# Contracting over 64-row tile pairs instead of 128-row passes in a fused attention and gated-FFN kernel

## The chip, the cores and the metric

The kernel runs on one core of one Trainium2 chip. Times are device microseconds of one execution. The numbers of a table or a sentence come from fast runs unless it says otherwise.

## The reference, cut to what matters

```python
# x: 2048 tokens x 576, bf16; 32 heads of 18; window of 256 keys, causal
xn = layernorm(x)
q, k, v = split(xn @ wqkv)                     # wqkv: 576 x 1728
o = softmax(mask(q @ k.T * 18**-0.5)) @ v      # per head
s = o @ wo                                     # wo: 576 x 576
h = sigmoid(xn @ w_gate) * (xn @ w_up)         # 576 x 4608 each
out = x + s * silu(h @ w_down)                 # w_down: 4608 x 576
```

The width 576 is what the change is about. It is four and a half times 128, so a contraction over it does not fill the kernel's passes of 128 rows (128\*128 in the profile's shapes) a whole number of times. It is nine times 64.

## The kernel before

A Python program builds a graph of operations, a list scheduler fixes their order on each engine from estimated durations, and the engines are ordered by semaphores. The tokens are processed in four chunks of 512. The attention of one chunk is interleaved with the FFN of the chunk before. Five ways of contracting matter here.

Gate/up takes two blocks of 128 columns at a time. Each block has four passes over 128 rows for gate and four for up. The remaining 64 rows are done as a pair of 64-row tiles: gate's on rows 0 to 63 of the array, up's on rows 64 to 127, at the same time (the two start 3 ns apart in the trace) and into two PSUM banks.

```python
for kt in range(4):                                     # main(): 128 rows
    eng.matmul(bank(h, w), wgs[:, sw, 4*w + kt, fc], x_in[:, kt, :], ...)
for w in range(2):                                      # rem(): 2 x 64 rows
    r = slice(64*w, 64*w + 64)
    eng.matmul(bank(h, w), wgs[r, sw, 8, fc], x_in[r, 4, :], ..., tile_position=(64*w, 0))

for fa in range(0, NFT, 2):                             # two blocks, fa and fb
    main(fa, ha, 0, True, ha); main(fa, ha, 1, True, None)
    rm = pe(..., rem of fa and rem of fb, [], hb)       # one piece, takes fb's PSUM unit
    tail(fa, ha, rm, rm)                                # tanh on ACT, product on DVE
    g = main(fb, hb, 0, ...); u = main(fb, hb, 1, ...)
    tail(fb, hb, g, u)
# ... cut
```

The projections q/k, v and wo pad 576 to five passes of 128 rows, with zeroed weights in the last one. V and wo have 576 output columns, done as 512 + 64. PV contracts 128 keys per pass into 19 columns. The down projection has 36 full passes of 128 rows per token block, each as 512 + 64 columns. The scores contract 18 rows per head and use four row tiles of 32 rows at once (in the trace all four start within 10 ns).

The softmax here doesn't subtract the row's maximum and nothing guards it: scores larger than these inputs give would overflow.

Of the kernel before, what the change touches and what calls it, by code (L numbers as in the profile page):

```python
# [13 lines left out]
KT = 5  # L14
# [12 lines left out]
UNIT = 18  # L27
NUNIT = 2 * H
NVB = 8
NQS = 4  # L30
NEX = 4
NXR = 4
# [11 lines left out]
def mm_ns(n):  # L44
    return max(25.0, n / 2.4 + 2.7)


def act_ns(n):
    return n / 1.2 + 175.0

# [53 lines left out]
class Op:  # L104
    __slots__ = ("eng", "est", "deps", "fn", "name", "prio", "start", "end", "tok", "needs_tok",
                 "nbytes", "idx", "succs", "cidx", "odeps", "acq", "lane")

    def __init__(self, eng, est, fn, name, deps, prio, nbytes, odeps, acq):
# [27 lines left out]
        self.lane = None  # L136
        for d in self.odeps:
            assert d.eng == eng
# [22 lines left out]
class Builder:  # L161
# [32 lines left out]
    def alloc_memory(self):  # L194
# [17 lines left out]
        self.xnT, _ = seq("xnT", [P, 2, KT, NT])  # L212
# [6 lines left out]
        self.kT, _ = seq("kT", [P, 2, NHG, NT])  # L219
        self.expr, zex = seq("expr", [P, NEX, 4, NT])  # L220
        self.stage = nc.alloc_sbuf_tensor_at("stage", [P, KT, 2 * D], bf16, offset=zex)
        assert size([P, KT, 2 * D], bf16) <= size([P, NEX, 4, NT], bf16)
        self.o_tok, _ = seq("o_tok", [P, BPC * D + 64])
        self.oT, _ = seq("oT", [P, 2, KT, P])
        self.s_attn, _ = seq("s_attn", [P, 2 * BPC, D])
        self.wqk, _ = seq("wqk", [P, KT, 2 * D])
        self.wv_sb, _ = seq("wv_sb", [P, KT, D])
        self.wo_sb, _ = seq("wo_sb", [P, KT, D])
        self.qd, _ = seq("qd", [P, NQD, 2, NT])
        self.xr, _ = seq("xr", [P, NXR, D])  # L230
        self.xnr, _ = seq("xnr", [P, NXN, KT * P])
# [8 lines left out]
        self.rstd, _ = seq("rstd", [P, NST, 1], f32)  # L240
        self.rrec, _ = seq("rrec", [P, 2, 4 * BPC], f32)
# [7 lines left out]
    def build_graph(self):  # L249
# [6 lines left out]
        self.r_rec = Ring(2, "rrec")  # L256
        self.r_oT = Ring(2, "oT")
# [24 lines left out]
        for c in range(NC):  # L282
            self.build_ln(c)
            self.build_v(c)
            made = 0
            for hg in range(NHG):
                need = min(NQK, (8 * UNIT * (hg + 2) - 1) // (2 * P) + 1)
                while made < need:
                    self.build_qk(c, made)
                    made += 1  # L290
                self.build_attn(c, hg)
            self.build_wo(c)
            self.build_ffn(c)

    def load_x(self, c):
        for i in range(0, BPC, 2):
            st = c * BPC + i
            slots, dd = [], []
            for _ in range(2):
                s_, d_ = self.r_xr.produce()  # L300
                slots.append(s_)
                dd += d_
            assert slots[1] == slots[0] + 1
            if c == 0:
                for j in range(2):
                    self.x_dma[st + j] = (self.dma(self.xr[:, slots[j], :], self.x[(st + j) * P:(st + j + 1) * P, :],
                                                   P * D * 2, f"dma:x{st + j}", ("x0", st + j), prio=0), slots[j])
            else:
                o = self.dma(self.xr[:, slots[0]:slots[0] + 2, :],
                             self.x[st * P:(st + 2) * P, :].rearrange("(t p) d -> p t d", p=P),  # L310
                             2 * P * D * 2, f"dma:x{st}", ("x", slots[0]), deps=dd, prio=0)
                for j in range(2):
                    self.x_dma[st + j] = (o, slots[j])

    def build_consts(self):
# [6 lines left out]
        z1 = op("POOL", 400, lambda e: e.memset(self.wqk[64:128, KT - 1, :], 0.0), "init:wqkz", deps=[self.op_ident], prio=1)  # L322
        z2 = op("POOL", 400, lambda e: e.memset(self.wv_sb[64:128, KT - 1, :], 0.0), "init:wvz", deps=[z1], prio=1)
        z3 = op("POOL", 400, lambda e: e.memset(self.wo_sb[64:128, KT - 1, :], 0.0), "init:woz", deps=[z2], prio=1)
        self.op_vones = op("POOL", 600, lambda e: e.memset(self.v_aug[:, :, :, DH:DH + 1], 1.0), "init:vones", deps=[z3], prio=1)
        self.op_opad = op("POOL", 200, lambda e: e.memset(self.o_tok[:, BPC * D:], 0.0), "init:opad", deps=[self.op_vones], prio=1)
        o2 = op("POOL", 500, lambda e: e.memset(self.mask[:, :, :], 1.0), "init:m0", deps=[self.op_opad], prio=1)
        ms = [o2]
        for i in range(4):
# [3 lines left out]
            else:  # L333
# [5 lines left out]
        sa = self.dma(self.stage[:, 0:4, :], self.wqkv[0:512, 0:2 * D].rearrange("(kt p) c -> p kt c", p=P),  # L339
                      4 * P * 2 * D * 2, "dma:stage", ("stage", 0), prio=2)  # L340
        sb = self.dma(self.stage[0:64, 4, :], self.wqkv[512:576, 0:2 * D], 64 * 2 * D * 2, "dma:stage4",
                      ("stage", 1), prio=2)
        va = self.dma(self.wv_sb[:, 0:4, :], self.wqkv[0:512, 2 * D:3 * D].rearrange("(kt p) c -> p kt c", p=P),
                      4 * P * D * 2, "dma:wv", ("wv", 0), prio=2)
        vb = self.dma(self.wv_sb[0:64, 4, :], self.wqkv[512:576, 2 * D:3 * D], 64 * D * 2, "dma:wv4",
                      ("wv", 1), prio=2)
        self.op_wv = [va, vb, z2]
        wa = self.dma(self.wo_sb[:, 0:4, :], self.wo[0:512, :].rearrange("(kt p) c -> p kt c", p=P),
                      4 * P * D * 2, "dma:wo", ("wo", 0), prio=8)
        wb = self.dma(self.wo_sb[0:64, 4, :], self.wo[512:576, :], 64 * D * 2, "dma:wo4", ("wo", 1), prio=8)  # L350
        self.op_wo_w = [wa, wb, z3]
        self.op_wqk = [z1]
        for kt in range(KT):
            def f_pack(eng, kt=kt):
                rows = P if kt < KT - 1 else 64
                dst = self.wqk[0:rows, kt, :].rearrange("p (g w c) -> p w g c", w=2, c=72)
                src = self.stage[0:rows, kt, :].rearrange("p (w g c) -> p w g c", w=2, g=NHG)
                return eng.activation(dst, src, ACTF.Copy)
            self.op_wqk.append(op("ACT", act_ns(2 * D), f_pack, f"pack:{kt}", deps=[sa if kt < 4 else sb], prio=2))

    def build_ln(self, c):
        op = self.op
        xs = c % 2
        if c > 0:
            self.load_x(c)
        war = self.xnT_rel[c - 2] if c >= 2 else []
        for i in range(BPC):
            st = c * BPC + i
            o_x, sx = self.x_dma[st]
            ss, ds = self.r_st.produce()  # L370
            b1 = op("DVE", 430, lambda e, ss=ss, sx=sx: e.bn_stats(self.bnst[:, ss, 0, :], self.xr[:, sx, 0:288]),
                    f"ln:bn1:{st}", deps=[o_x, ds], prio=0)
            b2 = op("DVE", 430, lambda e, ss=ss, sx=sx: e.bn_stats(self.bnst[:, ss, 1, :], self.xr[:, sx, 288:576]),
                    f"ln:bn2:{st}", deps=[o_x, ds], prio=0)
            ag = op("DVE", 200, lambda e, ss=ss: e.bn_aggr(self.mv[:, ss, :], self.bnst[:, ss, :, :]),
                    f"ln:ag:{st}", deps=[b1, b2], prio=0)
            ve = op("DVE", 140, lambda e, ss=ss: e.tensor_scalar(self.veps[:, ss, :], self.mv[:, ss, 1:2], EPS, None,
                                                                ALU.add), f"ln:ve:{st}", deps=[ag], prio=0)
            rs = op("POOL", 560, lambda e, ss=ss: e.tensor_tensor(self.rstd[:, ss, :], self.veps[:, ss, :],
                                                                  self.neghalf[:, :], ALU.pow),  # L380
                    f"ln:rs:{st}", deps=[ve, self.op_negh], prio=0)
            sn, dn = self.r_xn.produce()
            ap = op("DVE", 430, lambda e, ss=ss, sx=sx, sn=sn: e.tensor_scalar(
                self.xnr[:, sn, 0:D], self.xr[:, sx, :], self.mv[:, ss, 0:1], self.rstd[:, ss, :],
                ALU.subtract, ALU.mult), f"ln:ap:{st}", deps=[rs, ag, dn], prio=0)
            dup = op("DVE", 110, lambda e, sn=sn: e.tensor_copy(self.xnr[:, sn, D:KT * P], self.xnr[:, sn, 4 * P:D]),
                     f"ln:dup:{st}", deps=[ap], prio=0)
            self.r_xr.release(sx, ap)
# [3 lines left out]
            def f_tr(eng, h=h, sn=sn):  # L392
                b = h.units[0] * 2048
                res = None
                for kt in range(KT):
                    res = eng.transpose(self.psb[:, b + kt * P:b + (kt + 1) * P], self.xnr[:, sn, kt * P:(kt + 1) * P],  # L396
                                        self.ident[:, :])
                return res
            tr = op("PE", 5 * 60, f_tr, f"tr:{st}", deps=[dup, self.op_ident, war], prio=0, acq=h)
            self.r_xn.release(sn, tr)  # L400

            def f_xe(eng, h=h, i=i, xs=xs):
                b = h.units[0] * 2048
                src = self.psb[:, b:b + 5 * P].rearrange("p (k c) -> p k c", k=KT)
                return eng.activation(self.xnT[:, xs, :, i * P:(i + 1) * P], src, ACTF.Copy)
            xe = op("ACT", act_ns(5 * P), f_xe, f"xe:{st}", deps=[tr], prio=0)
            h.release(xe)
            self.op_xnT[c].append(xe)

    def build_qk(self, c, gi):  # L410
        op = self.op
        xs = par = c % 2
        ts = [t for t in (2 * gi, 2 * gi + 1) if t < 9]
        n = len(ts)
# [3 lines left out]
        def f_pj(eng):  # L418
            b = h.units[0] * 1024
            res = None  # L420
            for i, t in enumerate(ts):
# [8 lines left out]
        def f_ev(eng):  # L430
            b = h.units[0] * 1024
            return eng.tensor_copy(self.qd[:, sq, 0:n, :].rearrange("p t n -> p (t n)"), self.ps[:, b:b + n * 512])  # L432
# [533 lines left out]
```

## Time and profile before

The median is 635.8 us in three runs (635.67 to 637.77). These lines are from the page of the kernel before: the span, part 1 (busy time of the engines), the first line of part 4 (the chain of work that ended last), and four groups of part 5. PE is the tensor engine and PEld its weight loads, DVE the vector engine, ACT the scalar engine, POOL GpSimd; PSUM, `ps` in the lines, is where the matmuls' sums go; the program divides it into banks. A group's line has source line, engine and operation, then output and inputs, shapes, count, busy time, mean duration in ns, and the idle time of the engine just before.

```profile
span 634.0 us, 13361 instructions
...
PE 606.4 (96%) x5652; PEld 285.0 (45%) x5652; DVE 284.6 (45%) x493; ACT 290.8 (46%) x302; POOL 160.2 (25%) x320
...
PE 90%; ACT 3%; DVE 3%; issue 2%; DMA 1%; SPq 1%; DVEq 0%
...
L691 PE MATMUL ps<-xnT,wgs 128*128 128x512 bf16 x1152 | 273.2, 381 | 6.6 <-DVE hT L710 4.5
...
L749 PE MATMUL ps<-wd_sb,hT 128*128 128x512 bf16 x576 | 149.1, 380 | 0.0
...
L701 PE MATMUL ps<-xnT,wgs 64*128 64x512 bf16 x288 | 43.6, 381 | 0.3 <-DVE thf L774 0.3
L566 PE MATMUL ps<-v_aug,expr 128*128 128x19 bf16 x1440 | 41.1, 171 | 1.7 <-DVE hT L710 1.0
```

The tensor engine is busy for 96% of the span and it is 90% of the chain. The 1152 durations of 381 ns add up to 439 us, but they cover only 273.2 us of busy time: they overlap. So what a matmul costs in a stream is taken here as the distance from its start to the next start, and that has to be read from the times of the instructions. This is the timeline of the tensor engine in an undisturbed stretch of gate/up. The columns are start, duration, engine, line, operation, shapes and how many were merged.

```profile
521.14 0.60 PE L701 MATMUL ps<-xnT,wgs 64*128 64x512 bf16 x4
521.68 3.63 PE L691 MATMUL ps<-xnT,wgs 128*128 128x512 bf16 x16
525.24 0.60 PE L701 MATMUL ps<-xnT,wgs 64*128 64x512 bf16 x4
525.78 3.63 PE L691 MATMUL ps<-xnT,wgs 128*128 128x512 bf16 x16
529.34 0.61 PE L701 MATMUL ps<-xnT,wgs 64*128 64x512 bf16 x4
```

From one remainder to the next it is 4.10 us, for 16 passes of 128 rows and two pairs of 64-row tiles. Eighteen passes of 215.7 ns are 3.88 us. The other 0.21 us are at the two changes of tile size, from 128 rows to 64 and back (about 312 ns from start to start at each instead of 216, and 226 at the next).

These are the waits of the tensor engine, longest first (who waited for whom, us in total, times, longest).

```profile
PE ps L396 <- DVE xnr L386: 10.1, 3, 8.8
PE ps L691 <- DVE hT L710: 4.5, 5, 1.0
PE ps L525 <- DVE o_tok L589: 2.1, 7, 0.3
PE ps L691 <- ACT xnT L405: 2.1, 1, 2.1
```

The first and the fourth are the start of the program. The second is a PSUM wait in the middle: five times gate/up waited up to 1.0 us for `hT`, the product of the two banks, before it could take the PSUM unit again. The timeline of all engines shows how one of these came about (idle time before an instruction and what ended it in brackets).

```profile
195.85 1.88 ACT L541 ACTIVATE expr<-ps 128x2048 bf16<-128x2048 f32 x1 [1.07 <-PE ps L525]
...
196.27 1.90 PE L691 MATMUL ps<-xnT,wgs 128*128 128x512 bf16 x8
197.62 1.08 ACT L707 ACTIVATE tring<-ps 128x512 bf16<-128x512 f32 x2
...
198.10 0.40 PE L525 MATMUL ps<-qT,kT 18*128 18x256 bf16 x12
...
198.63 1.28 DVE L710 SCALAR_TENSOR_TENSOR hT<-tring,ps 128x512 bf16<-128x512 bf16 x2
...
199.46 0.81 PE L691 MATMUL ps<-xnT,wgs 128*128 128x512 bf16 x3 [0.96 <-DVE hT L710]
```

The tanh of the first block stood behind the exp of the attention until 197.6 us. By then the second block's tanh was due as well, so two tanh and two products ran one after the other, and PE stood still for 0.96 us.

### The profile page before, as it was taken

How to read it: one execution, taken by the hardware profiler on the slowest of the kernel's cores; microseconds unless marked ns; L12 is line 12 of the kernel's file. 1: busy time of each engine (PE TensorE's matmuls, PEld its weight loads, DVE VectorE, ACT ScalarE, POOL GpSimd, SP SyncE). 2: the span in 40 equal slices, each digit the busy share in tenths (PEclk: the TensorE clock that was granted, in tenths of full speed). 3: DMA queues.
4: the chain of work that ended last, by engine and by line, in shares of the span. 5: the costliest groups of instructions: out<-in, count | busy, mean ns of one | idle time of the engine just before them, and what ended most of it. 6: DMA issues, size and time to landing. Idle time of an engine off the chain costs nothing.

```text
span 634.0 us, 13361 instructions
## 1 busy us (share of the span) xinstructions
PE 606.4 (96%) x5652; PEld 285.0 (45%) x5652; DVE 284.6 (45%) x493; ACT 290.8 (46%) x302; POOL 160.2 (25%) x320
## 2 busy tenths in 40 slices
PE   2999999999999999999999999999999999999996
PEld 1444334355444444544555445344445543333453
DVE  3664545453455545524455454445544433333122
ACT  3524564561456647335654572656647322223100
POOL 5273506115550520255207005550340000000000
PEclk9999999999999999999999999999999999999999
DMA  8937655521113442334201133343340005553010
GB/s 249 304 99 221 170 165 152 156 57 37 36 36 95 117 133 81 81 89 112 67 30 40 46 111 84 92 129 96 102 130 21 21 20 152 147 143 101 1 39 20
DMA packets 110220, 63.14 MB, mean 100 GB/s; under 512 B 12144, under 2 KB 107568, under 8 KB 110160
## 3 DMA queue, kind: packets, MB, share of 16 engines
q1 hardware_dynamic: 100944, 57.53, 32.1%
q0 software_dynamic: 9216, 4.75, 2.8%
q8 instruction: 45, 0.74, 0.5%
q14 instruction: 15, 0.12, 0.1%
HBM read 55.15 MB, written 2.36 MB: 91 GB/s over the span
## 4 chain that ended last, share of the span: by engine, by line
PE 90%; ACT 3%; DVE 3%; issue 2%; DMA 1%; SPq 1%; DVEq 0%
PE ps L691 39%; PE ps L749 20%; PE ps L423 6%; PE ps L566 5%; PE ps L701 5%; PE ps L525 5%; PE ps L471 3%; ACT expr L541 3%; PE ps L629 3%; PE ps L751 3%; DMA stage<-in_A_wqkv_dram 1%; DVE qd L432 1%; PE ps L607 1%; PE ps L396 1%; DVE hT L710 1%
## 5 line engine op out<-in xcount | busy, mean ns | idle before, releaser
L691 PE MATMUL ps<-xnT,wgs 128*128 128x512 bf16 x1152 | 273.2, 381 | 6.6 <-DVE hT L710 4.5
L541 ACT ACTIVATE expr<-ps 128x2048 bf16<-128x2048 f32 (+1 forms) x96 | 170.1, 1771 | 73.6 <-PE ps L525 72.8
L691 PEld LDWEIGHTS ps<-xnT,wgs 128*128 128x128 bf16 x1152 | 101.7, 98 | 145.1 <-issue 38.7
L707 ACT ACTIVATE tring<-ps 128x512 bf16<-128x512 f32 x144 | 85.3, 597 | 141.3 <-PE ps L701 122.4
L749 PE MATMUL ps<-wd_sb,hT 128*128 128x512 bf16 x576 | 149.1, 380 | 0.0
L710 DVE SCALAR_TENSOR_TENSOR hT<-tring,ps 128x512 bf16<-128x512 bf16 x144 | 98.3, 686 | 94.7 <-ACT tring L707 61.4
L549 DVE TENSOR_TENSOR expr<-expr,mask 128x1536 bf16<-128x1536 bf16 (+2 forms) x96 | 79.2, 825 | 129.2 <-ACT expr L541 129.1
L190 POOL DMA_DIRECT2D qT<-qd x144 | 73.1, 514 | 213.5 <-DVE rrec L581 109.3
L751 PE MATMUL ps<-wd_sb,hT 128*128 128x64 bf16 x576 | 111.0, 193 | 0.0
L749 PEld LDWEIGHTS ps<-wd_sb,hT 128*128 128x128 bf16 x576 | 56.2, 98 | 67.1 <-issue 3.8
L190 POOL DMA_DIRECT2D kT<-qd x144 | 72.7, 511 | 52.7 <-DVE rrec L581 18.7
L751 PEld LDWEIGHTS ps<-wd_sb,hT 128*128 128x128 bf16 x576 | 56.4, 98 | 0.4
L566 PEld LDWEIGHTS ps<-v_aug,expr 128*128 128x128 bf16 x1440 | 40.3, 96 | 9.9 <-DVE expr L549 1.9
L701 PE MATMUL ps<-xnT,wgs 64*128 64x512 bf16 x288 | 43.6, 381 | 0.3 <-DVE thf L774 0.3
L566 PE MATMUL ps<-v_aug,expr 128*128 128x19 bf16 x1440 | 41.1, 171 | 1.7 <-DVE hT L710 1.0
L423 PE MATMUL ps<-xnT,wqk 128*128 128x512 bf16 x180 | 42.0, 379 | 0.0
L525 PE MATMUL ps<-qT,kT 18*128 18x256 bf16 (+1 forms) x960 | 37.0, 245 | 2.2 <-DVE o_tok L589 2.1
L432 DVE CAST qd<-ps 128x1024 bf16<-128x1024 f32 (+1 forms) x20 | 22.4, 1118 | 32.5 <-PE ps L423 32.3
L772 ACT ACTIVATE thf<-ps 128x576 bf16<-128x576 f32 x16 | 10.4, 650 | 52.4 <-PE ps L751 52.4
L525 PEld LDWEIGHTS ps<-qT,kT 18*128 18x128 bf16 x960 | 15.6, 92 | 38.3 <-issue 11.7
L774 DVE SCALAR_TENSOR_TENSOR thf<-thf,ps 128x576 bf16<-128x576 bf16 x16 | 12.0, 752 | 45.5 <-ACT thf L772 45.5
L640 ACT ACTIVATE s_attn<-ps 128x576 bf16<-128x576 f32 x16 | 10.4, 652 | 42.8 <-PE ps L632 42.8
(46 smaller groups left out, 246.4 us busy)
## 6 DMA issues: line engine op xcount, KB each, us to landing
wgs<-in_B_w_gate_dram SPq DMA_DIRECT2D x72, 256.0 KB, 3.0
wgs<-in_B_w_up_dram SPq DMA_DIRECT2D x72, 256.0 KB, 3.6
wd_sb<-in_B_w_down_dram SPq DMA_DIRECT2D x9, 576.0 KB, 5.4
wgs<-in_B_w_gate_dram SPq DMA_DIRECT2D x72, 32.0 KB, 3.0
wgs<-in_B_w_up_dram SPq DMA_DIRECT2D x72, 32.0 KB, 3.1
xf<-in_A_x_dram SPq DMA_DIRECT2D x16, 144.0 KB, 2.1
out_dram<-xf SPq DMA_DIRECT2D x16, 144.0 KB, 1.8
qT<-qd POOLq DMA_DIRECT2D x112, 18.0 KB, 2.2
```

Source lines behind the costliest of these rows:

```text
L190: o = self.op(eng, DMA_ISSUE_NS[eng], lambda e: e.dma_start(dst, src), name, deps, prio, nbytes=nbytes)
L423: res = eng.matmul(self.ps[:, b + i * 512:b + (i + 1) * 512], self.wqk[:, kt, t * P:(t + 1) * P], self.xnT[:, xs, kt, :], start=(kt == 0), ...
L525: res = eng.matmul(self.ps[:, o:o + nq * P], self.kT[r, kp, hg, ko:ko + P], self.qT[r, qs, q0 * P:(q0 + nq) * P], start=True, stop=True, t ...
L541: return eng.activation(dst, src, ACTF.Exp, scale=SM_SCALE)
L549: return eng.tensor_tensor(e_, e_, m_, ALU.mult)
L566: res = eng.matmul(self.ps[:, o:o + 19], self.expr[:, se, h4, at * P:(at + 1) * P], self.v_aug[:, kb % NVB, hg * 4 + h4, :], start=(n == 0 ...
L691: res = eng.matmul(bank(h, w), self.wgs[:, sw, 4 * w + kt, fc], x_in[:, kt, :], start=(first and kt == 0), stop=(not first and kt == 3))
L701: res = eng.matmul(bank(h, w), self.wgs[r, sw, 8, fc], x_in[r, 4, :], start=first, stop=not first, tile_position=(64 * w, 0))
L707: th = op("ACT", act_ns(NT), lambda e: e.activation(self.tring[:, st, :], bank(h, 0), ACTF.Tanh, scale=0.5), f"th:{c}:{ft}", deps=[pg, dt_ ...
L710: mu = op("DVE", dve_ns(NT), lambda e: e.scalar_tensor_tensor(self.hT[:, ft, :], self.tring[:, st, :], 1.0, bank(h, 1), ALU.add, ALU.mult) ...
L749: eng.matmul(self.ps[:, b:b + 512], self.hT[:, ft, cols], self.wd_sb[:, ft, 0:512], start=(ft == 0), stop=(ft == NFT - 1))
L751: res = eng.matmul(self.ps[:, b + 512:b + 576], self.hT[:, ft, cols], self.wd_sb[:, ft, 512:576], start=(ft == 0), stop=(ft == NFT - 1))
```

## The change

The intent is that everything on the tensor engine except the scores and the down projection uses one tile size. A contraction over 576 becomes nine passes; each pass is a pair of 64-row tiles that run side by side into two banks. Gate is on rows 0 to 63 and up on rows 64 to 127; likewise q and k, and the two column halves of v and wo. In the program each tile takes its operands from the partitions with the numbers of its rows (`ROWS[t]` in `pair`). So both halves of the partitions hold all nine blocks of x (and of o), and x is transposed from a copy with its first 64 columns repeated at the end. PV sums its 128 keys as two halves in two banks, and DVE adds the two. Here is the core of the diff:

```diff
+def pair(eng, outs, lhs, rhs, start, stop):
+    for t in range(2):
+        res = eng.matmul(outs[t], lhs(ROWS[t], t), rhs(ROWS[t], t), start=start, stop=stop, tile_position=(64 * t, 0))
...
-        self.xnT, _ = seq("xnT", [P, 2, KT, NT])          # KT = 5
+        self.xnT, _ = seq("xnT", [P, 2, KS, NT])          # KS = 9
...
+    def load_rows(self, dst, lo, hi, name, lane, prio, deps=()):   # weights: 64 partitions per DMA
+        for t, src in enumerate((lo, hi)):
+            w = src.rearrange("(s p) c -> p s c", p=64)
+            for o in range(2): ... self.dma(dst[ROWS[t], k0:k0 + len(sub), :], w[:, o:KS:2, :], ...)
...
-        for fa in range(0, NFT, 2):                        # two blocks at a time, see above
-            ...
+        for ft in range(NFT):                              # one block at a time
+            h = self.pool_f.hold()
+            gate_up(ft, h, 0, h)                           # 5 pairs
+            u = gate_up(ft, h, 1, None)                    # 4 pairs
+            tail(ft, h, u)
...
-                        res = eng.matmul(self.ps[:, o:o + 19], self.expr[:, se, h4, ...], self.v_aug[:, ...], ...)
+                        res = pair(eng, [b[:, o:o + 19] for b in outs], ...)          # PV
+        sm = op("DVE", dve_ns(608), f_sum, f"ps:{c}:{hg}", deps=[pv, dp], prio=1)
...
-            o = pe(FG * (mm_ns(512) + 28), f_f2, ...)      # down: 512 + 64 columns
+            o = pe(FG * 2 * mm_ns(288), f_f2, ...)         # down: 288 + 288 columns
+            o.mode = 128
```

Cut from it: q/k weights are loaded directly, where before they were packed on ACT from a staging tile; three memsets go; the rings of `kT`, `s_attn` and x become shorter; the LayerNorm of later chunks gets a lower priority; the scores wait for their `expr` slot before they take PSUM; and the scheduler adds 95 ns where the tile size changes.

## The prediction

> **What bounds the kernel now.** The tensor engine. The page's first part has PE busy 606.4 us of 634.0 (96%), DVE, ACT and POOL at 45%, 46% and 25%. The chain of waits is 90% PE. PE idles before about 14.9 us (timeline), 6 us at the end, some 10 between. So the time is the sum of the matmuls' start-to-start spacings in the trace:
> - 512 columns 215.7 ns; 64 columns 29; 128-column transposes 56; PV (19 columns) 25.2.
> - Row tiles: the scores' four row tiles start 3 to 4 ns apart and a group of 128 columns repeats after 56 ns, like one matmul. Gate/up's two 64-row remainder tiles start 3 ns apart. So a pair costs one matmul.
> - From 128-row to 64-row tiles takes 312 ns instead of 216, back 308 instead of 212, and the first group after it 10 ns more: about 106 ns a switch. [...]
>
> **Removed.**
> 1. Gate/up's mode switches around its remainder. Undisturbed, the stage repeats every 4.095 us for 18 passes, alone 3.88. With pairs only (still 1296 passes): 72 x 0.213 = -15.3 us.
> 2. Padding of K to 5 x 128: q/k 180 passes of 216 ns (38.9 us) become 144 of 216 and 36 of 109 (35.0): -3.9. V and wo: 32 x 5 x (216 + 29) = 39.2 become 32 x 9 x 122.7 = 35.3: -3.9. Transposes 9.0 to 8.4.
> 3. Start: packing wqk on ACT (5.5 us) and three POOL memsets, which held the first rstd from 4.7 to 7.2 us. Steady PE work starts 2 to 3 us earlier.
>
> **Unchanged.** Down projection: 512 + 64 columns take 244.5 ns, 288 + 288 about 245. Switches around the scores stay.
>
> **Added.**
> - PV: 1440 passes of 25 ns become 1440 pairs. Score groups do four weight loads and matmuls in 56 ns, so a pair should take 25 to 29: I take +1 us. If each instruction cost 25 ns: +36, the main risk.
> - The down projection stays at 128 rows while q/k, transposes and PV become 64: some 30 new switches of 0.1 us: +3.
> - Summing PV's banks on DVE (32 x about 0.7 us) and wider copies after transposes (32 x 0.3 to 0.5 us): some 30 us on DVE and ACT, off the chain. Shorter rings for s_attn, kT, x. +2 for new waits.
>
> **Critical path.** PE terms lie on it one for one: -15.3 - 8.4 - 2.5 + 1 + 3 + 2 = about -20.
>
> **Prediction: 615 us, range 604 to 626 (8 in 10).** Faster by over 2% (below 623): 0.78; within 2%: 0.18; slower: 0.04.
>
> **What would show each step.** Undisturbed gate/up repeats every 3.88 us per two blocks with no change of shape; q/k, V and wo total about 70 us of spacing instead of 78; PV pairs repeat every 25 to 29 ns, the two matmuls 3 ns apart; down projection still 245 ns; steady PE work from about 12.5 us; DVE busy over 300 us, PE's waits below 15 us in all.
>
> **What would make it wrong.** PV pairs that serialise (50 ns); sustained 64-row pairs slower than the short bursts seen here (10 ns each would cost 13 us); more switches during the down projection; waits on DVE or ACT in attention; weights arriving late in the first chunk, where DMA is busiest.

The spacings for 256 and 288 columns (109 and 122 to 123 ns) are estimates; they lie on the straight line through the 29 ns of 64 columns and the 215.7 ns of 512 in the trace of before.

## The result

The change took the time from 636.57 to 617.26 us (medians of four runs each; 616.6 to 622.16 after), a ratio of 0.9712 with a 95% interval of 0.9658 to 0.9766. A second set of runs, in a later round, gave 617.0 us (616.47 to 618.05) and 0.9698 (0.9683 to 0.9713). The output was correct. A ratio in this text is the mean time of one kernel's fast runs over that of the kernel before in the same rounds on the same chip, so it is not quite the ratio of the medians quoted beside it.

These are the lines of the page after that answer to those shown of before. L59 is the line of the helper `pair`, so a group has to be told by its tiles.

```profile
span 615.8 us, 20345 instructions
...
PE 593.2 (96%) x9096; PEld 338.9 (55%) x9096; DVE 312.5 (51%) x529; ACT 293.0 (48%) x297; POOL 157.8 (26%) x316
...
PE 88%; ACT 5%; issue 2%; DVE 2%; DMA 1%; SPq 1%
...
L59 PE MATMUL ps<-xnT,wgs 64*128 64x512 bf16 x2592 | 298.8, 376 | 1.4 <-DVE hT L713 1.2
...
L744 PE MATMUL ps<-wd_sb,hT 128*128 128x288 bf16 x1152 | 151.4, 287 | 0.0
...
L59 PE MATMUL ps<-v_aug,expr 64*128 64x19 bf16 x2880 | 41.3, 168 | 0.1
```

The number of gate/up instructions went from 1440 to 2592, and the engine's busy time for them fell from about 317 to 299 us: pairs do run side by side. PV doubled its instructions at the same busy time. DVE gained 28 us of work, of which the new sum of the PV banks is 25.3 us. The engine that bounds the kernel is the same one.

This is the timeline of the tensor engine in the undisturbed stretch, and in a stretch with attention.

```profile
203.95 2.12 PE L59 MATMUL ps<-xnT,wgs 64*128 64x512 bf16 x18
206.15 1.16 PE L59 MATMUL ps<-xnT,wqk 64*128 64x256 bf16 x18
207.15 1.36 PE L59 MATMUL ps<-v_aug,expr 64*128 64x19 bf16 x96
208.36 7.93 PE L59 MATMUL ps<-xnT,wgs 64*128 64x512 bf16 x72
...
507.82 64.48 PE L59 MATMUL ps<-xnT,wgs 64*128 64x512 bf16 x596
```

The second line to the fourth are q/k, PV and gate/up in a row with no idle time and no change of tile size between them. From 207.15 to 208.36 the 48 PV pairs took 1.21 us, or 25.2 ns each. In the last line nothing interrupts gate/up any more. By the instructions' start times two blocks repeat every 3.885 us there, where the prediction said 3.88.

### Where the 18 us came from

To go further I split the span of each trace in the same way. From the first pass that is not a transpose of x on, every pass (one matmul, one pair, or one group of four) has a nominal spacing, 25.2 ns for PV and for the others the value on a straight line through the spacings of the two traces: 2.4 ns and 0.4167 ns for each column. That is 29.1, 55.7, 109.1, 122.4 and 215.7 ns for 64, 128, 256, 288 and 512 columns; the medians of the streams are 29, 56, 109, 123 and 216. What a spacing has above that, up to 110 ns, counts as a switch if the next pass has another tile size, and so do the 10 ns that the first pass after a switch takes longer. All else is waiting. The method has one weakness: a short wait that falls on a switch is counted as part of the switch.

| us, profiled runs | before | after | difference |
|---|---|---|---|
| until steady work starts | 14.9 | 15.3 | +0.4 |
| nominal passes | 562.4 | 554.1 | -8.3 |
| switches (number) | 34.4 (317) | 26.9 (243) | -7.5 |
| waits | 16.6 | 13.7 | -2.9 |
| after the last pass started | 5.7 | 5.8 | +0.1 |
| span | 634.0 | 615.8 | -18.2 |

The second profile of the kernel after has 14.8 + 554.1 + 26.8 + 14.7 + 5.8 = 616.2 us, so the waits of a run are good to about 1 us. The median switch costs 96 ns before and 100 ns after. What the engine does in that time is not shown.

The waits of the tensor engine after the change:

```profile
PE ps L420 <- DVE xnr L394: 7.0, 2, 6.3
PE ps L59 <- DMA wqk<-in_A_wqkv_dram: 5.1, 1, 5.1
PE ps L59 <- DVE hT L713: 1.2, 5, 0.3
```

Two things differ. The wait for `hT` fell from 4.5 us to 1.2 us, which nobody predicted. And 5.1 us are now spent on the load of `wqk`. x was ready at 11.4 us, when its last copy on ACT ended, but the first q/k pass started only at 15.34 us:

```profile
15.34 1.03 PE L59 MATMUL ps<-xnT,wqk 64*128 64x512 bf16 x4 [5.06 <-DMA wqk<-in_A_wqkv_dram]
```

The next view is busy time by engine in a stretch of the span, 8 to 24 us, with the granted clock, the share of the DMA engines' time and the rate at the end. First before:

```profile
8.00:24.00 16.00, 11.81 (x71) 5.66 (x71) 8.94 (x34) 9.81 (x12) 2.48 (x5) 1.00 1.06 309
```

And after:

```profile
8.00:24.00 16.00, 9.99 (x116) 6.17 (x118) 6.97 (x22) 3.92 (x5) 4.86 (x9) 1.00 1.15 221
```

The DMA engines have work all the time in both (the view gives shares of 1.06 and 1.15), but they move 221 GB/s instead of 309. So the time that the change took out of the start (packing, memsets) went into waiting for slower loads.

### The profile page after: what moved, and what is told of

It is laid out like the page before. It is cut to its first block, busy times and chain, and to the rows that moved or that the text cites. A ratio compares the mean times of both kernels' runs of the same rounds, so it can differ in the third digit from the quotient of the medians.

```text
span 615.8 us, 20345 instructions
## 1 busy us (share of the span) xinstructions
PE 593.2 (96%) x9096; PEld 338.9 (55%) x9096; DVE 312.5 (51%) x529; ACT 293.0 (48%) x297; POOL 157.8 (26%) x316
## 4 chain that ended last, share of the span: by engine, by line
PE 88%; ACT 5%; issue 2%; DVE 2%; DMA 1%; SPq 1%
PE ps L59 59%; PE ps L744 23%; PE ps L551 4%; ACT expr L568 4%; PE ps L420 1%; DMA wqk<-in_A_wqkv_dram 1%; SPq L202 1%; ACT tring L710 1%; DVE hT L713 1%; DVE thf L770 0%; DVE thf L773 0%; ACT xnT L408 0%; DVE xf L776 0%; DVE expr L576 0%; DVE pvs L606 0%
## 5 line engine op out<-in xcount | busy, mean ns | idle before, releaser
L59 PE MATMUL ps<-xnT,wgs 64*128 64x512 bf16 x2592 | 298.8, 376 | 1.4 <-DVE hT L713 1.2
L59 PEld LDWEIGHTS ps<-xnT,wgs 64*128 64x128 bf16 x2592 | 119.2, 94 | 144.6 <-issue 13.9
L744 PE MATMUL ps<-wd_sb,hT 128*128 128x288 bf16 x1152 | 151.4, 287 | 0.0
L202 POOL DMA_DIRECT2D qT<-qd x144 | 73.6, 511 | 258.1 <-DVE qd L457 187.2
L744 PEld LDWEIGHTS ps<-wd_sb,hT 128*128 128x128 bf16 x1152 | 107.9, 98 | 32.1 <-issue 4.5
L59 PE MATMUL ps<-xnT,wqk 64*128 64x512 bf16 (+1 forms) x360 | 40.2, 368 | 5.2 <-DMA wqk<-in_A_wqkv_dram 5.1
L59 PEld LDWEIGHTS ps<-v_aug,expr 64*128 64x128 bf16 x2880 | 40.1, 93 | 8.4 <-issue 2.9
L59 PE MATMUL ps<-v_aug,expr 64*128 64x19 bf16 x2880 | 41.3, 168 | 0.1
L457 DVE CAST qd<-ps 128x1024 bf16<-128x1024 f32 (+1 forms) x20 | 22.3, 1116 | 27.6 <-PE ps L59 27.6
L59 PEld LDWEIGHTS ps<-xnT,wqk 64*128 64x128 bf16 x360 | 17.3, 96 | 25.1 <-issue 7.5
L408 ACT ACTIVATE xnT<-ps 128x1152 bf16<-128x1152 bf16 x16 | 17.7, 1130 | 22.2 <-PE ps L420 22.2
L606 DVE TENSOR_REDUCE pvs<-ps 128x304 f32<-128x608 f32 x32 | 25.3, 790 | 4.9 <-PE ps L59 4.6
```

What stands on the lines that cost most here:

```text
L59: res = eng.matmul(outs[t], lhs(ROWS[t], t), rhs(ROWS[t], t), start=start, stop=stop, tile_position=(64 * t, 0))
L202: o = self.op(eng, DMA_ISSUE_NS[eng], lambda e: e.dma_start(dst, src), name, deps, prio, nbytes=nbytes)
L408: return eng.activation(dst, self.tr_src(h), ACTF.Copy)
L457: return eng.tensor_copy(dst, self.both(h, n))
L606: return eng.tensor_reduce(self.pvs[:, pt, :], self.both(hp, 304).rearrange("p t q -> p q t"), mybir.AxisListType.X, ALU.add)
L744: res = eng.matmul(outs[t], self.hT[:, ft, cols], self.wd_sb[:, ft, 288 * t:288 * t + 288], start=(ft == 0), stop=(ft == NFT - 1))
```

## The experiments

My theory was: the pass time is fixed by the shapes, each change of tile size costs about 0.106 us on the chain, and the rest is small. The rivals were that the gain comes from the removed padding and the rescheduling around it, that gate/up alone is the whole gain, that DVE's new sum costs something, and for the start that bytes, not their order, are the limit. The number of switches of each kernel was counted from its program before it ran.

### Gate/up put back

The edit to the kernel after (the loads of gate/up weights too go back to before's form):

```diff
-        for ft in range(NFT): ... gate_up(ft, h, 0, h); u = gate_up(ft, h, 1, None); tail(ft, h, u)
+        for fa in range(0, NFT, 2): ... main(fa, ...); rem of fa and fb; tail(fa, ...); main(fb, ...); tail(fb, ...)
-                    res = pair(eng, outs, lambda r, t: self.wgs[r, sw, k, fc], lambda r, t: x_in[r, k, :], ...)
+                    res = eng.matmul(bank(h, w), self.wgs[:, sw, 4 * w + kt, fc], x_in[:, kt, :], ...)
```

> The kernel after, with gate/up alone put back to 128-row passes and a 64-row remainder per two blocks; everything else stays as changed. Its program has 395 changes of tile size on the tensor engine, against 243 after and 317 before. If a change costs about 0.106 us and lies on the chain (my theory), the time is 617 + 152 x 0.106 = 633 us, and up to 638 if the waits of about 1 us for the gate/up product, of which before had five, come back with the paired blocks. If instead the gain came from the removed padding, the start and the scheduling of everything else (rival), most of it stays and the time is below 622.

It took 643.62 us (643.11 to 643.95), slower than the kernel before itself: ratio 1.0118 (1.0102 to 1.0135). Against the second profile of after, the switches rose by 16.0 us (26.8 to 42.8 for 152 more, 0.105 each) and the waits by 9.7 us (14.7 to 24.4), while nominal passes stayed at 554.1. The waits of the tensor engine in this kernel:

```profile
PE ps L708 <- DVE hT L729: 8.4, 12, 1.0
PE ps L420 <- DVE xnr L394: 7.0, 2, 6.3
PE ps L59 <- DMA wqk<-in_A_wqkv_dram: 3.9, 1, 3.9
```

The theory's term for the switches is confirmed. The rival, that the gain lies in all the rest, is wrong. The waits for `hT` came back in full and more (12.2 us in all, with two shorter lines of this view that are not shown), and took the time above my upper figure of 638. A kernel with q/k, v, wo and PV in one tile size and gate/up in another is worse than both the kernel before and the kernel after.

### Gate/up pairs alone

The edit to the kernel before: gate/up as in the change, `xnT` with nine blocks made by nine 128-row transposes, and the shorter `s_attn` and `kT`, without which it does not fit. The scheduler knows the switches.

```diff
-                for kt in range(KT):
+                for kt in range(KS):
+                    c0 = kt * P if kt < 5 else (kt - 5) * P + 64
-        for fa in range(0, NFT, 2): ...
+        for ft in range(NFT): ... gate_up(ft, h, 0, h); u = gate_up(ft, h, 1, None); tail(ft, h, u, u)
```

> The kernel before, with only gate/up turned into pairs of 64-row tiles (this needs nine 128-row transposes of x instead of five, and the smaller s_attn and kT rings of the change to fit). 273 changes of tile size against 317 before. My theory: 637 - 44 x 0.106 + 3.6 (64 more transposes of 56 ns) - up to 5 (waits) = 631 to 635 us; the pairs only pay once their neighbours use the same tile size. Rival: removing the 144 changes around the remainder is worth 15 us by itself, so 621 to 625.

It took 628.9 us (626.88 to 630.97), ratio 0.9877 (0.985 to 0.9904). That is 2 us below my range and 4 us above the rival's. The trace has 273 switches at 29.9 us (-4.5 against before), nominal passes +2.7, the start +3.2 (it waits for the v weights) and waits 10.3 us (-6.3). So gate/up alone gives about 40% of the gain, and what it gives comes as much from waits that vanished as from switches. The 144 switches around the remainder are not worth 15 us by themselves: only 44 switches went in all, because PV, q/k, v, wo and the transposes then stand in the other tile size.

### PV put back

```diff
-                        res = pair(eng, [b[:, o:o + 19] for b in outs], ...)
+                        res = eng.matmul(self.ps[:, o:o + 19], self.expr[:, se, h4, at * P:(at + 1) * P], ...)
-        sm = op("DVE", dve_ns(608), f_sum, f"ps:{c}:{hg}", deps=[pv, dp], prio=1)
```

> The kernel after, with PV alone put back to one 128-row pass into one bank, and the sum of the two banks on DVE (25 us busy) gone. 273 changes of tile size against 243. My theory: PV passes cost the same 25 ns, so 617 + 30 x 0.106 = 620.5 us. Rival: the pair or its sum costs time that the removed changes don't pay back, then this kernel is as fast as after or faster, 614 to 617.

It took 618.56 us (617.99 to 619.46), ratio 0.9726 (0.9709 to 0.9744), against 0.9698 (0.9683 to 0.9713) for the kernel after: 0.3% or nearly 2 us slower, but the two intervals still touch. The profile has 3.0 us more of switches and 3.7 us fewer waits than the second profile of after, and its span (615.9 us) is that of after (615.8 and 616.2 us). So the sign of the medians is what the theory said, the size is about half, and what PV in pairs saves in switches it largely gives back in waits. That the pair and its sum pay at all is not shown; that they cost no more than they give is.

### The kernel after once more

> The changed kernel once more, unaltered, for a narrow interval on the same chip as the next three: 616.5 to 618 us, with a rare run some us higher.

617.0 us (616.47 to 618.05), as given above. It is the yardstick. The next two kernels and the combination of them ran on the same chip; the others ran on other chips, each set with the kernel before beside it, and are compared by their ratios.

### Down projection in pairs too

After the change the down projection is the only stage beside the scores with another tile size. In pairs, each output bank would need both halves of the contraction. I kept two row tiles from writing one bank at the same time; no run here tried what that does. So two token blocks are interleaved: each bank gets its second row tile only after a pass over the other block.

```diff
+        for i in range(0, BPC, 2):
+            hs = [self.pool_f.hold() for _ in range(2)]
+            p1 = [half(i + k, hs[k], 0, None) for k in range(2)]        # rows 0-63 -> bank 0, 64-127 -> bank 1
+            for k in range(2):
+                self.build_final(c * BPC + i + k, hs[k], half(i + k, hs[k], 1, p1[k]))   # the other way round
```

> The kernel after, with the down projection in pairs of 64-row tiles too, two token blocks interleaved so that each bank changes its row tile only after a long-finished pass (and the transposes of o wait for their oT slot, against a deadlock of the rings). 192 changes of tile size, all around the scores, against 243. Theory that a change costs 0.106 us on the chain: 617 - 51 x 0.106 = 612 us. Rival, that these changes are hidden or that 288-column pairs run slower than two 288-column passes: 616 or more.

It took 617.87 us (616.15 to 622.6), ratio 0.9722 (0.9694 to 0.975). The theory, applied as it stood, failed. The switches did fall by 5.0 us (26.8 to 21.8), the passes took the same time (down projection 147.8 us in total, against 148.0), and the waits rose by 4.1 us (14.7 to 18.8). Part of this can be seen in single spacings. Leaving the down projection for work of the same tile size cost 2.5 us in this kernel for 26 times; leaving it with a switch cost 2.8 us for 25 times in the kernel after; and in the kernel before, without a switch, 2.2 us for 25 times. By place: from the down projection to PV most spacings have about 0.17 us above nominal, with a switch or without; to q/k 0.10 with and 0.08 without; to gate/up and wo 0.10 with and mostly nothing without. So towards PV and q/k taking away the switch took away little or none of the extra time. My reading, which no run tests by itself, is that the switch and a wait of about the same length overlapped there. Towards gate/up and wo the extra time of the switch went, but here four of the eight steps to the transposes waited 0.25 to 0.35 us each. Together these waits on leaving the down projection are 2.2 of the 4.1 us. Only the way back was clearly cheaper (2.4 us of switches after, none here). The rest of the waits is scattered (0.4 us of it before the first down projection); I did not isolate it.

### The start: order of work, order of loads, and two queues

Four kernels try to regain the 2 to 3 us that the start was to give. The first changes the scheduler's idea of the DMA rate, so that gate/up comes before q/k.

```diff
-DMA_BYTES_PER_NS = 280.0
+DMA_BYTES_PER_NS = 175.0
```

> The kernel after, with one constant of its build-time scheduler changed, the assumed DMA rate from 280 to 175 bytes per ns, so that gate/up instead of q/k comes first on the tensor engine at the start. After waited 5.1 us for the wqk load, until 15.3 us, though x was ready at 11.4. If the load order of the program is the cause, steady work starts at about 11.5 to 12 us and the time falls by 3 to 4 us, to 613 to 614 (238 changes of tile size instead of 243 give 0.5 of it). If the start is bound by DMA whatever comes first, nothing changes: 617.

Steady work did start at 11.6 us, 3.2 us earlier than in the yardstick. Yet the time was 622.49 us (617.69 to 624.08), ratio 0.9771 (0.9743 to 0.9799): slower. The timeline of the tensor engine shows what happened later in the first chunk, since attention now came later:

```profile
46.40 1.21 PE L420 MATMUL ps<-ident,xnr 64*128 64x64 bf16 x36 [1.97 <-DVE xnr L394]
47.42 3.55 PE L59 MATMUL ps<-xnT,wgs 64*128 64x512 bf16 x18
...
54.64 0.40 PE L551 MATMUL ps<-qT,kT 18*128 18x128 bf16 x12 [1.01 <-ACT expr L568]
...
57.02 2.12 PE L59 MATMUL ps<-xnT,wqk 64*128 64x512 bf16 x18 [0.80 <-ACT expr L568]
```

Three waits of 0.8 to 2.0 us appeared, and nine passes after the first of them took 3.55 us instead of the 2.12 us of the q/k passes with the same shape. The view by stretches says why; the third number from the end is the granted clock:

```profile
47.40:49.60 2.20, 2.20 (x20) 0.81 (x16) 0.00 (x0) 1.63 (x2) 0.00 (x0) 0.50 1.21 182
```

The clock of the tensor engine was granted at half (0.50), in this trace from 46.94 to 50.36 us. That begins 2.5 us after the last pass of gate/up ended: 1.97 us of idle time, and nine pairs of transposes still at full speed (29 ns apart; the next nine were 53 ns apart). The half speed itself lasted 3.4 us. What sets it off is not shown, and a wait of about 2 us alone did not do it in every trace: the kernel with the down projection in pairs had a wait of 2.2 us, and its clock stayed at 1.0 there. The other runs of this kernel had mean clocks of 0.990 to 0.996, against 0.997 to 1.0 for the yardstick, which fits, but only this one was profiled.

Both edits together, pairs in the down projection and this scheduler constant:

> Both the last two edits together. If both theories hold they add: 617 - 5.4 - 3.5 = 608 us. If the earlier start only moves a wait to later in the first chunk, where DMA is busiest, 611 to 612.

619.28 us (617.84 to 620.96), ratio 0.9733 (0.9714 to 0.9752). The earlier start was there (11.5 us), the switches were down (21.8 us), and the waits were 24.1 us. This trace too has 3.4 us at half clock, from 49.1 us. The two edits do not add.

Next, the order of the loads alone. The order on the tensor engine and the number of switches stay as after.

```diff
-            wk[:, 0:512], "dma:wqk", ("wqk", 0), 2)
+            wk[:, 0:512], "dma:wqk", ("wqk", 0), 1)      # before the first gate/up weights
```

> The kernel after, with the load of wqk issued before the first gate/up weights (one priority changed); the order of work on the tensor engine and its 243 changes of tile size stay the same. After waited until 15.3 us for wqk. 0.59 MB at the 220 GB/s of that stretch are 2.7 us, so steady work starts at about 12.6 us and the time falls to 614 to 615 if the start is on the chain. If the first chunk is bound by the bytes that must arrive by 28 us, in whatever order, PE waits later instead: 617.

617.03 us (616.28 to 618.22), ratio 0.9705 (0.9687 to 0.9723): the same. The waits of the tensor engine say where it went:

```profile
PE ps L59 <- DMA wv_sb<-in_A_wqkv_dram: 1.8, 1, 1.8
PE ps L59 <- DMA wqk<-in_A_wqkv_dram: 1.7, 1, 1.7
```

The 5 us wait was split into one for `wqk` and one for `wv`. The passes have the same order as in the yardstick, so they can be compared one by one: steady work started at 12.0 us, 2.8 us earlier, and at the 19th pass, at 19.9 us, the lead was gone. This is what the second expectation said: the bytes are the limit, not their order.

Why do the same bytes come more slowly? The change loads every weight tile as four DMAs, each into one half of the partitions. This table is worked out from the packet records of the traces: the mean time of one 512-byte packet, a gate/up weight row, in the first 28 us and in the rest (for the kernel after, in its second profile).

| kernel | gate/up weights go to | 0 to 28 us | later |
|---|---|---|---|
| before | 128 partitions | 31 ns | 29 ns |
| before, gate/up pairs alone | 64 partitions | 34 ns | 31 ns |
| after, gate/up put back | 128 partitions | 33 ns | 29 ns |
| after | 64 partitions | 42 ns | 33 ns |

Packets of this size that went into half of the partitions were slower in both pairs of kernels: at the start 34 against 31 ns in the kernel before and 42 against 33 ns in the kernel after, later 31 and 33 against 29 ns. (The figure varies: the first profile of after has 41 ns at the start, the kernel with wqk first 44.) Why is not shown. My prediction named late weights as a risk and did not cost the layout. The change also shortened the rows of the other first loads, which no run separates from this: wqk came in rows of 2304 bytes before and comes in rows of 1024 and 128 after, wv in 1152 before and 576 after. A 2304-byte packet took 115 ns before, a 1024-byte packet 79 ns after, so fewer bytes per ns here too (13 instead of 20). To test the layout, the first loads into the upper half were issued from ScalarE's queue, so that both halves could be written at once:

```diff
-                res.append(self.dma(dst[ROWS[t], ...], ..., prio=prio))
+                res.append(self.dma(dst[ROWS[t], ...], ..., prio=prio, eng=hi_eng if t else "SP"))   # hi_eng="ACT" for the first loads
```

> The kernel after, with the first loads into partitions 64 to 127 (gate/up of the first eight blocks, wqk, wv) issued from ScalarE's queue and those into 0 to 63 from SyncE's, so that both halves are written at once. In the first 28 us a 512-byte packet took 42 ns after and 31 ns before. Theory, loads that fill one half of the partitions at a time are slower for it: packets go back to 31 to 35 ns, the rate in 8 to 24 us rises from 220 to about 280 GB/s, the wqk wait shrinks by 2 us or more and the time falls to 614 to 615. Rival, the layout is not the cause: 42 ns, 220 GB/s and 617.

The packets took 37 ns, against 42 in the second profile of after. The stretch from 8 to 24 us of this kernel:

```profile
8.00:24.00 16.00, 11.09 (x140) 6.07 (x138) 7.74 (x24) 6.41 (x7) 4.19 (x8) 1.00 1.19 260
```

The rate rose to 260 GB/s, from 221 and 225 in the two profiles of after. That is a good part of what the theory asked for, not all. The time was 616.32 us (615.47 to 616.84), ratio 0.9692 (0.9677 to 0.9708): perhaps 0.5 us better than the yardstick and not separated from it. The `wqk` wait is gone, but issuing eleven DMAs on ScalarE delayed its first copies of x, and PE waited for those instead (3.3 and 1.3 us). So it is likely that the layout is part of the slower loading; a control with two queues and without the split into halves was not run. How much time it costs is not shown.

> Both load edits together: wqk first, and the two halves from two queues. If both theories hold, steady work from 11.5 to 12 us (x is ready at 11.4) and 613 to 614; if only the load order counts 614 to 615; if neither, 617.

616.49 us (615.64 to 617.69), ratio 0.9696 (0.9677 to 0.9715). Steady work started at 13.9 us, and again no clear gain.

### One block or two at a time

The waits for `hT` fell with the change and came back with gate/up put back. There the tile size and the order of the blocks changed together. This experiment keeps the pairs and all 243 switches, and restores only the order and the pieces of before.

```diff
-            gate_up(ft, h, 0, h); u = gate_up(ft, h, 1, None); tail(ft, h, u)
+            gate_up(fa, ha, range(0, 4), ha); gate_up(fa, ha, range(4, 8), None)
+            rm = pe(..., last pass of fa and first pass of fb, [], hb); tail(fa, ha, rm)
+            gate_up(fb, hb, range(1, 5), None); u = gate_up(fb, hb, range(5, 9), None); tail(fb, hb, u)
```

> The kernel after, all in 64-row pairs, but gate/up's passes in the order and the pieces of before: two blocks at a time, with the last pass of the first and the first pass of the second issued as one piece that takes both PSUM units. 243 changes of tile size as in after. With gate/up as before (128 rows) the trace had 10 us more of waits than after, besides 16 us of changes. Theory: the two-block order causes those waits, because two tanh then stand behind one exp on ACT; then this kernel takes 623 to 627 us. Rival: the waits come from the tile changes themselves or from the scheduler's estimates of them; then 617.

It took 620.77 us (619.35 to 627.21), ratio 0.9777 (0.9744 to 0.981), which does not overlap the yardstick's interval (it was measured on another chip, and the interval of the first set of after, 0.9658 to 0.9766, does overlap). The waits for `hT`:

```profile
PE ps L59 <- DVE hT L713: 4.6, 8, 1.1
...
PE ps L753 <- DVE hT L713: 0.7, 1, 0.7
```

They are 5.3 us in all and up to 1.1 us long, against 1.2 us in the first profile of after and 2.8 in the second. So the block order by itself makes long waits, and by the medians it costs some 3 to 4 us. The profiled run, the fastest of the six, shows 1.4 to 1.8 us of that in its span. It is not the 6 to 10 us that I had expected. The kernel with gate/up put back has this same block order and 152 switches more, and its ratio is higher by 0.034, or 22 us; 16 us of these are the switches themselves. The rest, with `hT` waits of 12.2 instead of 5.3 us, comes with the 128-row gate/up in some way that stays open.

### Down projection in pairs with both load edits

> Candidate for a better version: down projection in pairs plus both load edits. 192 changes of tile size. The three edits gave nothing clear alone (617.9, 617.0 and 616.3 us against 617.0). If the time is now bound by the waits between engines, it stays at 615.5 to 617; if the edits had only hidden each other's gain, they add up to 611 to 613.

615.31 us in the median; its fast runs are 613.75 to 619.23, and one slow run took 623.89. The ratio is 0.969 (0.9663 to 0.9716). Its profile is the shortest of all (612.0 us, with 21.8 us of switches and 16.5 of waits), but the interval contains the yardstick's. I do not claim a better kernel than the changed one.

## Why the prediction was right, point by point

- **The bound.** Right. PE has 88% of the chain after, and the time is again the sum of the spacings.
- **A pair costs one pass.** Right, and the risk of slower sustained pairs did not come: 1116 of 1197 gate/up spacings without a neighbour of another kind are at 216 ns within 3 ns.
- **Padding of K.** Right by the count of passes: nominal passes fell by 8.3 us, 8.4 were predicted; no run put the padding back alone. The measured spacings of q/k, V and wo together fell from 79.9 to 73.6 us. q/k as a whole fell by 2.1 us instead of 3.9, because the slow passes at the very start of the work, 427 ns apart, now fall into q/k instead of gate/up and v.
- **PV, +1 us.** Right: 38.0 us of spacing before, 38.1 after. The check named beforehand, two matmuls 3 ns apart, holds for half of the pairs (732 of 1440 within 4 ns); in nearly all others they start about 20 ns apart, and the pair takes 25 ns all the same.
- **Down projection unchanged.** Right for the passes (141 us nominal in both).
- **Switches, -15.3 and +3.** Too large: -7.5 us. The remainder of gate/up had 144 switches in the sum, but 19 of them led straight to or from the scores, where a switch stays; 125 went. Around the down projection 51 came instead of 30. That leaves 74 fewer, and 317 - 243 is just that. In the table the new ones count with nearly 5 us. Net they cost less, since the 25 ways out of the down projection already cost 2.2 us of waits before, without a switch.
- **Start, -2.5 us.** This step failed: "Steady PE work starts 2 to 3 us earlier" became 0.4 us later in the first profile and 0.1 us earlier in the second. The work before it was removed as said (x was ready at 11.4 us), but the loads, now into 64 partitions and in part with shorter rows, ran at 221 instead of 309 GB/s. The kernels that did start 1 to 3 us earlier (at 11.6, 12.0 and 13.9 us) lost it again within the first chunk or were not separated from the yardstick.
- **New waits, +2 us.** The sign was wrong: -2.9 us. The change also made gate/up run one block at a time, which the prediction saw in the diff and did not cost. The experiment on it shows 3 to 4 us for that by its medians.

The predicted 615 us was met within 0.4%, but by terms that erred by up to 5 us in both directions; that these errors cancelled is luck. With the sizes measured here the sum is -8.3 - 7.5 - 2.9 + 0.4 + 0.1 = -18.2 us.

## What to carry to other kernels

Count the changes of tile size in the program before costing a tiling: each cost about 0.1 us here (medians of 96 and 100 ns), and a stage put into a new tile size gained much less where its neighbours in time did not share it (gate/up pairs alone gave some 40% of the gain, and gate/up put back alone is slower than both versions). Do not count the full cost of a change at a place where the engine may wait without it too (from the down projection to PV about 0.17 us above nominal, with a change or without). And when a layout splits the partitions into halves, look at what its loads do: here fewer preparing instructions did not start the kernel earlier, since its first bytes arrived more slowly (221 instead of 309 GB/s).
